# The last 64 rows of wq to 64 partitions, and the gate's weights in one transfer

## The chip, the cores and the metric

The kernel runs on one core of one Trainium2 chip. The metric is the device time of one execution in microseconds (us); lower is better. The times given are medians of several runs of the same program on the same chip, and the profile is of one further execution.

## The reference, cut to what matters

One decode step: attention of one query token over a cache of 65,536 positions (16 query heads, 8 key and value heads of size 256), mixed by a gate with a small token mixer.

```
x = A_x                                              # (1, 1, 448)
g = sigmoid((x * gate_w).sum(-1, keepdims=True))     # gate_w has 448 numbers

q = (x @ wq).reshape(16 heads, 256)                  # wq: 448 x 4096
p = softmax(q . k_cache * 256 ** -0.5)               # k_cache, v_cache: 8 x 65536 x 256, bf16
a = (p . v_cache) @ wo                               # wo: 4096 x 448

h = layernorm(x)
u = gelu(einsum("bsd,sf->bdf", h, w1) + b1)          # 448 x 1792
b = transpose(einsum("bdf,fs->bds", u, w2) + b2)

out = g * a + (1 - g) * b                            # 448 numbers, bf16
```

Keys and values are 268 MB each. They are read once and make up nearly all the bytes.

## The kernel before, in words

**The stream.** Keys and values are cut into 32 blocks (8 heads, 4 blocks each) of 16,384 positions. A block is 8.39 MB: 128 partitions with 128 rows of 256 numbers each, that is 64 KB in a row per partition. `load_k_whole` (line 132) fetches a block of K into two of the three slots of `k_all`, `load_v` (line 135) a block of V into `vt`. All these loads are issued on SyncE's queue. The loop (line 608 in the profile is the loop and the code that opens its stages) handles two blocks a round: transposes of K on VectorE (line 413), scores on PE (421), a running softmax (478 to 517), products with V on PE (441). In each round `load_wo_wide` (144) fetches 224 KB of wo to every fourth partition. After the loop the last two blocks are written out by hand, the last V block in seven pieces that get smaller (`LAST`, line 161), and the result is stored (708).

**Ahead of the loop.** The query is computed from wq, which lies in `vt` until the first V block takes its place. Rows 0 to 383 are `wq_m`, three rows to each of 128 partitions (issued at line 170). The last 64 rows are `wq_t` (issued at 167): each row of 4096 numbers is cut into two halves, so that 128 half rows of 4 KB fill 128 partitions. A partition then holds the half `half` of a row, and the 16 heads fall into two halves of 8. So that each head's product takes only the rows of its own half, x for these rows is prepared in two columns, `xtm`: x's last 64 numbers are written twice in a row (`xrr`, line 231, VectorE), a matmul with a one turns them into a column (240, PE), and a multiplication with the mask `par` (203), which is 1 on the partitions of the right parity, makes the two columns (248). The query's matmuls are at lines 300 (`wq_m`, three for each of 32 columns) and 307 (`wq_t`, one for each).

ScalarE's queue carries the small inputs: x (`xr`, line 166), three tables of the mixer (`tables`, 176), the gate's weights in two halves of 448 bytes (`gw`, 178), and `b2b` (181). The tables are turned by one matmul (262) and copied to `wb1` (272). VectorE makes the layernorm from a broadcast of x over all partitions (the matmul at 244; 265 to 284), with `veps` at 268. ScalarE computes 14 gelus (289) and the gate's exponential (351). Then the loop begins.

**What sets the order.** A helper, `seq`, ties every instruction to the one before it on the same engine, so each engine and each queue runs in the order in which the code is written. The framework adds the waits for data. It also gives each transfer outside the loop one of eight completion counters in turn; a transfer that takes a counter for the second time waits until the first one that used it has landed. The ten transfers ahead of the loop are x, wq_t, the three tables, wq_m, gw, gw, b2b and the first K block.

Of the kernel before, what the change touches and what calls it, by code (L numbers as in the profile page):

```python
# [8 lines left out]
FP32 = mybir.dt.float32  # L9
BF16 = mybir.dt.bfloat16  # L10
ACT = mybir.ActivationFunctionType
ALU = mybir.AluOpType
AXIS = mybir.AxisListType

HQ = 16
HKV = 8
DH = 256
REP = HQ // HKV
# [15 lines left out]
def kernel(  # L34
# [15 lines left out]
    nc = tc.nc  # L50

    D = A_x.shape[-1]
# [10 lines left out]
    def seq(ins):  # L63
        e = ins.ins.engine
        if e in last:
            tc.add_manual_dep(
                ins.ins,
                last[e],
                mybir.DependencyInfo(
                    mybir.DependencyClass.NoSync, mybir.DependencyReason.DATA  # L70
                ),
                reason="program order",
            )
        last[e] = ins.ins.name
        return ins

    kvpool = ctx.enter_context(tc.tile_pool(name="kvpool", bufs=1))
    const = ctx.enter_context(tc.tile_pool(name="const", bufs=1))
# [8 lines left out]
    vt = kvpool.tile([128, VP, DH], BF16, name="vt")  # L87
# [17 lines left out]
    xr = const.tile([1, D], BF16)  # L105
    gw = const.tile([1, D], BF16)
# [2 lines left out]
    b2b = const.tile([1, 1], BF16)  # L109
    DM = 384  # L110
    wq_m = vt[:, 0:48, :].rearrange("p a b -> p (a b)").rearrange("p (k n) -> p k n", k=3)
    wq_t = vt[:, 48:56, :].rearrange("p a b -> p (a b)")
    early = slots[2].rearrange("p j d -> p (j d)")
    gel = [early[:, b * D:(b + 1) * D] for b in range(NF)]
    early_f = early[:, NF * D:].bitcast(FP32)
# [43 lines left out]
    def load_v_last(n):  # L159
# [4 lines left out]
            ))  # L164

    seq(nc.scalar.dma_start(out=xr[:], in_=A_x[0, 0].rearrange("(o n) -> o n", o=1)))
    seq(nc.sync.dma_start(
        out=wq_t[:, :], in_=A_wq[DM:D, :].rearrange("r (h n) -> (r h) n", h=2)
    ))
    seq(nc.sync.dma_start(out=wq_m, in_=A_wq[0:DM, :].rearrange("(p k) n -> p k n", k=3)))  # L170
    for k, table in enumerate((
        B_w1[0].rearrange("(b p) -> b p", p=128),
# [1 line left out]
        B_w2.rearrange("(b p) o -> b (p o)", p=128),  # L174
    )):
        seq(nc.scalar.dma_start(out=tables[k * NF:(k + 1) * NF, :], in_=table))
    for n0, n1 in ((0, D // 2), (D // 2, D)):
        seq(nc.scalar.dma_start(
            out=gw[:, n0:n1], in_=gate_w.rearrange("(o n) -> o n", o=1)[:, n0:n1]
        ))  # L180
    seq(nc.scalar.dma_start(out=b2b[:], in_=B_b2.rearrange("(o n) -> o n", o=1)))
    load_k_whole(0, 0)

# [5 lines left out]
    ident_f = const.tile([128, 128], FP32)  # L189
# [4 lines left out]
        out=val[:], in_=rowsel[:, :, :, 0:NI], op=ALU.add, axis=AXIS.XY  # L194
# [3 lines left out]
        out=fst[:],  # L198
        in_=ident_f[:].rearrange("p (a i r) -> p i r a", a=4, r=REP)[:, 0:2],
        op=ALU.add, axis=AXIS.X,  # L200
    ))
    par = const.tile([128, REP], FP32)
    seq(nc.vector.tensor_reduce(
        out=par[:], in_=ident_f[:].rearrange("p (a r) -> p r a", r=REP), op=ALU.add, axis=AXIS.X
    ))
    nval = const.tile([128, REP], FP32)
    seq(nc.scalar.mul(out=nval[:], in_=val[:], mul=-scale))
# [6 lines left out]
        out=same[:], in_=val[:].unsqueeze(1).to_broadcast([128, 64, REP])  # L214
# [8 lines left out]
        out=sel[:],  # L223
        in_=ident.rearrange("p (w k) -> p w k", w=NW).unsqueeze(2).to_broadcast([128, NW, NQ, 32]),
# [1 line left out]


    xm = const.tile([128, 3], BF16)
    xtm = const.tile([128, REP], BF16)
    xrr = const.tile([1, D - DM, 2], BF16)  # L230
    seq(nc.vector.tensor_copy(
        out=xrr[:], in_=xr[:, DM:D].unsqueeze(2).to_broadcast([1, D - DM, 2])
    ))
    x_col = hd_ps[:, 40:44]
    for k in range(3):
        seq(nc.tensor.matmul(
            x_col[:, k:k + 1], lhsT=xr[:, 0:DM].rearrange("o (p k) -> o k p", k=3)[:, k, :],
            rhs=ones_b[:, 0:1], start=True, stop=True,
        ))
    seq(nc.tensor.matmul(  # L240
        x_col[:, 3:4], lhsT=xrr[:].rearrange("o a r -> o (a r)"),
        rhs=ones_b[:, 0:1], start=True, stop=True,
    ))
    seq(nc.tensor.matmul(
        sm_ps[:, 0:D], lhsT=ones_b[:, :], rhs=xr[:, :], start=True, stop=True
    ))
    seq(nc.vector.tensor_copy(out=xm[:], in_=x_col[:, 0:3]))
    seq(nc.vector.tensor_scalar(
        out=xtm[:], in0=par[:], scalar1=x_col[:, 3:4], scalar2=None, op0=ALU.mult
    ))  # L250


    stats = work.tile([128, nc.vector.BN_STATS_DIM], FP32)
# [9 lines left out]
        t_ps, lhsT=tables[:, :], rhs=ident[0:3 * NF, 0:3 * NF], start=True, stop=True  # L263
# [5 lines left out]
        out=veps[:], in0=mv[:, 1:2], scalar1=1e-5, scalar2=None, op0=ALU.add  # L269
# [5 lines left out]
    for _ in range(2):  # L275
        seq(nc.vector.scalar_tensor_tensor(
            out=ntmp[:], in0=rstd[:], scalar=rstd[:, 0:1], in1=veps[:],
            op0=ALU.mult, op1=ALU.mult,
        ))
        seq(nc.vector.tensor_scalar(  # L280
            out=ntmp[:], in0=ntmp[:], scalar1=-0.5, scalar2=1.5, op0=ALU.mult, op1=ALU.add
# [3 lines left out]
        out=h_bc, in0=xf, scalar1=mv[:, 0:1], scalar2=rstd[:, 0:1],  # L285
        op0=ALU.subtract, op1=ALU.mult,
    ))
    for b in range(NF):
        seq(nc.scalar.activation(
            out=gel[b], in_=h_bc, func=ACT.Gelu_apprx_tanh,  # L290
# [2 lines left out]

    q_ps = hd_ps[:, 0:2 * HQ]
    for h in range(HQ):
        half, hh = divmod(h, HQ // 2)
        for c in range(2):
            col = c * HQ + h
            for k in range(3):
                seq(nc.tensor.matmul(  # L300
                    q_ps[:, col:col + 1],
                    lhsT=wq_m[:, k, h * DH:(h + 1) * DH].rearrange("p (d c) -> p c d", c=2)[:, c, :],
                    rhs=xm[:, k:k + 1],
                    start=(k == 0),
                    stop=False,
                ))
            seq(nc.tensor.matmul(
                q_ps[:, col:col + 1],
                lhsT=wq_t[:, hh * DH:(hh + 1) * DH].rearrange("p (d c) -> p c d", c=2)[:, c, :],
                rhs=xtm[:, half:half + 1],  # L310
                start=False,
                stop=True,
            ))
# [3 lines left out]
    for w in range(NW):  # L317
        seq(nc.tensor.matmul(
            qq_ps[:, w * 2 * HQ:(w + 1) * 2 * HQ],
            lhsT=sel[:, w, :, :].rearrange("p a k -> p (a k)"), rhs=qb[:],  # L320
# [3 lines left out]
    for k in range(2):  # L324
        seq(nc.vector.tensor_copy(
            out=qq[:, :, :, k, :], in_=qq_ps.rearrange("p (w g r) -> p w g r", g=HKV, r=REP)
# [316 lines left out]
    for n in (L - 1, L):  # L643
# [14 lines left out]
        else:  # L658
            def rest_base():
# [9 lines left out]
                out=lsv[:], in0=val[:], scalar1=lsum[:, 0:1], scalar2=None, op0=ALU.mult  # L669
# [8 lines left out]
                out=rdv[:], in0=rdv[:], scalar1=gcol[:, 0:1], scalar2=None, op0=ALU.mult  # L678
# [6 lines left out]
    for c in range(2):  # L685
        for e in range(2):
            seq(nc.tensor.matmul(
                o_last[:, c, :],
                lhsT=acc[:, e, :].rearrange("p (d c) -> p c d", c=2)[:, c, :],
                rhs=fst[:, e, :],  # L690
# [4 lines left out]
        out=oT[:], in0=o_last, in1=rdv[:].unsqueeze(1).to_broadcast([128, 2, REP]), op=ALU.mult  # L695
    ))
    for r in range(REP):
        for c in range(2):
            for k in range(2):
                seq(nc.tensor.matmul(  # L700
                    f_rows[k], lhsT=oT[:, c, r:r + 1],
                    rhs=wo_sb[:, r, c, k * MC:(k + 1) * MC],
# [36 lines left out]
```

## Time and profile before

| | |
|---|---|
| median of 3 runs | 1263.77 us (1263.45 to 1264.1) |
| the profiled execution: its time | 1264.05 us |
| its span, first to last instruction | 1262.3 us |
| moved | 544.35 MB, mean 431 GB/s |
| TensorE clock granted, mean | 0.817 |
| busy share of the span | PE 65%, VectorE 56%, PE's weight loads 26%, ScalarE 6%, GpSimd 1% |

The profile is of one execution. Its time is 1.75 us more than its span; the difference lies around the first and the last instruction. Times in rows of the timeline count from the span's start. A row of the timeline gives start, duration, engine, line, operation, output and inputs, how many, and in brackets how long the engine sat idle before it and what ended that. "q" behind an engine's name is its sequencer, which issues DMAs; the duration of such a row is that of the issue, not of the transfer. The DMA share is the mean busy share of the core's 16 DMA engines; since a packet is counted where its time falls or ends, a short stretch can show more than 1.

### The profile page before, as it was taken

The numbers are of one execution on the slowest core, as the hardware profiler recorded it, in microseconds if no ns is written. First come the engines' busy times: TensorE is split into PE (matmuls) and PEld (weight loads), VectorE is DVE, ScalarE is ACT, GpSimd is POOL, SyncE is SP. The second block draws the span as 40 slices with busy tenths as digits, with TensorE's granted clock in tenths as the row PEclk, the third lists the DMA queues.
The fourth block names the chain that finished last, engine by engine and source line by source line (L and its number), as shares of the span: only waits on it lengthen the run. The fifth ranks groups of instructions, "written<-read, shape, count | busy, mean of one in ns | idle before, by whom it ended". The sixth has DMA issues, their size and how long they took to land.

```text
span 1262.3 us, 12389 instructions
## 1 busy us (share of the span) xinstructions
PE 816.7 (65%) x4818; PEld 329.8 (26%) x4818; DVE 705.4 (56%) x733; ACT 78.2 (6%) x170; POOL 7.7 (1%) x21
## 2 busy tenths in 40 slices
PE   5757567574676756677564766658666586565668
PEld 2222222231222212222222322213222132222224
DVE  3665456664556644566444665446654456654575
ACT  5000000000000000000000000000000000000000
POOL 2000000000000000000000000000000000000000
PEclk8787788778888877878779887788887788877979
DMA  9999999999999999999999999999999999999998
GB/s 416 432 435 432 439 432 432 439 432 427 438 438 418 447 416 436 430 437 436 435 432 439 432 432 439 432 439 432 432 439 432 439 432 432 439 432 435 423 431 357
DMA packets 11623, 544.35 MB, mean 431 GB/s; under 512 B 1532, under 2 KB 1918, under 8 KB 2782
## 3 DMA queue, kind: packets, MB, share of 16 engines
q1 hardware_dynamic: 11522, 544.22, 99.6%
q8 instruction: 6, 0.10, 0.0%
q10 hardware_dynamic: 92, 0.01, 0.0%
q14 instruction: 3, 0.02, 0.0%
HBM read 544.22 MB, written 0.00 MB: 431 GB/s over the span
## 4 chain that ended last, share of the span: by engine, by line
DMA 69%; PE 13%; DVE 12%; issue 4%; SPq 0%; ACT 0%; DVEq 0%
DMA k_all<-in_A_k_cache_dram 67%; PE sc L421 12%; DVE kT L413 12%; DMA k_all<-in_A_v_cache_dram 2%; PE pv_last L566 0%; PE hd_ps L557 0%; PE f L566 0%; PE f L700 0%; PE sm_ps L543 0%; PE hd_ps L466 0%; ACT p_sb L509 0%; DVE rmax L478 0%; SPq L132 0%; PE hd_ps L543 0%; PE sm_ps L496 0%
## 5 line engine op out<-in xcount | busy, mean ns | idle before, releaser
L421 PE MATMUL sc<-kT,qz 128*128 128x512 bf16 x2048 | 546.8, 417 | 324.4 <-DVE kT L413 324.3
L413 DVE STREAM_TRANSPOSE kT<-k_all 128x2048 f32<-128x2048 f32 x256 | 570.9, 2283 | 211.6 <-DMA k_all<-in_A_k_cache_dram 161.1
L421 PEld LDWEIGHTS <-qz 128*128 128x128 bf16 x2048 | 211.7, 103 | 658.3 <-issue 479.6
L441 PE MATMUL pv_ps<-vt,pT 128*4 128x512 bf16 x1968 | 166.9, 513 | 27.3 <-DVE pT L516 27.3
L522 DVE SCALAR_TENSOR_TENSOR acc<-acc,al,pv_ps 128x512 f32<-128x512 f32 x31 | 23.2, 747 | 155.4 <-PE pv_ps L441 155.4
L441 PEld LDWEIGHTS <-pT 128*4 128x4 bf16 x2000 | 55.7, 106 | 125.9 <-issue 77.1
L509 ACT ACTIVATE p_sb<-sc,nb 128x512 bf16<-128x512 f32 x32 | 22.0, 687 | 1023.6 <-DVE nb L505 1023.6
L478 DVE TENSOR_REDUCE rmax<-sc 128x1 f32<-128x512 f32 x32 | 22.1, 691 | 63.7 <-PE sc L421 63.7
L516 DVE STREAM_TRANSPOSE pT<-p_sb 128x512 bf16<-128x512 bf16 x32 | 22.8, 711 | 27.1 <-ACT p_sb L509 27.1
L528 PE MATMUL hd_ps<-lsum,same 128*128 128x1 f32 x30 | 7.6, 322 | 28.8 <-DVE lsum L517 28.8
L496 PE MATMUL sm_ps<-mrun,ones_f 1*128 1x2 f32 x64 | 12.1, 257 | 21.2 <-DVE mrun L495 13.0
L482 PE MATMUL sm_ps<-ident_f,rmax 128*1 128x128 f32 x32 | 8.6, 270 | 24.6 <-DVE rmax L478 24.6
L566 PE MATMUL pv_last<-wo_in,steps 128*128 128x448 bf16 x64 | 15.6, 368 | 3.8 <-PEq L608 3.8
L566 PEld LDWEIGHTS <-steps 128*128 128x128 bf16 x128 | 11.6, 101 | 20.9 <-issue 12.7
L561 DVE TENSOR_TENSOR a_acc<-a_acc,hd_ps 1x448 f32<-1x448 f32 x15 | 9.1, 609 | 14.0 <-PE hd_ps L557 14.0
L496 PEld LDWEIGHTS sm_ps<-mrun,ones_f 1*128 1x128 f32 x64 | 9.4, 183 | 27.5 <-DVE mrun L495 16.4
L557 PE MATMUL hd_ps<-wo_sb,oT 128*1 128x448 bf16 x60 | 16.4, 365 | 0.0
L570 ACT CAST wo_sb<-pv_last 128x448 bf16<-128x448 f32 x16 | 8.5, 532 | 122.5 <-PE pv_last L566 122.5
L566 PE MATMUL f<-wo_in,steps 128*128 128x448 bf16 x64 | 15.5, 367 | 0.0
L573 ACT COPY wo_sb<-wo_sb 128x896 bf16<-128x896 bf16 x15 | 14.1, 937 | 15.3 <-PE hd_ps L557 15.3
L528 PEld LDWEIGHTS hd_ps<-lsum,same 128*128 128x128 f32 x30 | 6.3, 262 | 30.1 <-DVE lsum L517 30.1
L553 DVE CAST oT<-hd_ps 128x2 bf16<-128x2 f32 x15 | 2.4, 159 | 21.0 <-PE hd_ps L543 21.0
(123 smaller groups left out, 196.1 us busy)
## 6 DMA issues: line engine op xcount, KB each, us to landing
k_all<-in_A_k_cache_dram SPq DMA_DIRECT2D x2, 4096.0 KB, 15.9
vt<-in_A_v_cache_dram SPq DMA_DIRECT2D x1, 5120.0 KB
k_all<-in_A_v_cache_dram SPq DMA_DIRECT2D x1, 4096.0 KB
wo_in<-in_A_wo_dram SPq DMA_DIRECT2D x15, 224.0 KB, 27.8
vt<-in_A_wq_dram SPq DMA_DIRECT2D x1, 3072.0 KB, 10.4
vt<-in_A_v_cache_dram SPq DMA_DIRECT2D x1, 3072.0 KB
k_all<-in_A_v_cache_dram SPq DMA_DIRECT2D x1, 2048.0 KB
k_all<-in_A_v_cache_dram SPq DMA_DIRECT2D x1, 1024.0 KB, 22.3
```

What stands on the lines that cost most here:

```text
L413: seq(nc.vector.transpose(out=kT_tiles[i % 2][:].rearrange("p j w k c -> p (j w k c)").bitcast(FP32), in_=slots[pair[i // 4]][:, i % 4 * N ...
L421: seq(nc.tensor.matmul(sc_tiles[e][:, :], lhsT=qz[:, 2 * w + c, 2 * (NI - i):2 * (NI - i) + 128], rhs=kT_tiles[i % 2][:, :, w, :, c], star ...
L441: seq(nc.tensor.matmul(dst[32 * grp:32 * grp + 2 * REP, :, :], lhsT=pT[:, 32 * jj + 2 * REP * ip:32 * jj + 2 * REP * (ip + 1)], rhs=pairs( ...
L478: seq(nc.vector.tensor_reduce(out=rmax[:], in_=sc_ps[:, :], op=ALU.max, axis=AXIS.X))
L496: seq(nc.tensor.matmul(sm_ps[:, 128:128 + REP], lhsT=ones_f[0:1, :], rhs=mrun[0:1, :], start=True, stop=True))
L509: seq(nc.scalar.activation(out=p_sb[:, :], in_=sc_ps[:, :], func=ACT.Exp, scale=scale, bias=nb[:, 0:1], accum_out=den[:, 0:1],))
L516: seq(nc.vector.transpose(out=pT[:, :], in_=p_sb[:, :]))
L522: seq(nc.vector.scalar_tensor_tensor(out=acc[:], in0=acc[:], scalar=al_tiles[e][:, 0:1], in1=src[:, :, :], op0=ALU.mult, op1=ALU.add,))
L528: seq(nc.tensor.matmul(hd_ps[:, 460:461], lhsT=same[:].rearrange("p a r -> p (a r)"), rhs=lsum[:, 0:1], start=True, stop=True,))
L557: seq(nc.tensor.matmul(a_ps, lhsT=oT[:, c, r:r + 1], rhs=wo_sb[:, r, c, :], start=(r == 0 and c == 0), stop=(r == REP - 1 and c == 1),))
L566: seq(nc.tensor.matmul(wo_ps[c], lhsT=steps[:, WS - u:WS - u + 128], rhs=wo_in[:, 2 * u + c, :], start=(u == 0), stop=(u == WS - 1),))
L573: seq(nc.scalar.copy(out=wo_sb[:, 0], in_=wo_sb[:, 1]))
```

## The change

The last 64 rows of wq are loaded as they are: 64 rows of 8 KB to partitions 0 to 63, in twice the columns of `vt`. The contraction over them then needs one column of x, `xt`, on 64 partitions: x goes into its matmul directly, and the copy `xrr`, the mask `par` and the multiplication fall away. The 32 query matmuls at what was line 307 contract over 64 rows instead of 128. The gate's weights come in one transfer of 896 bytes instead of two of 448. There are nine transfers ahead of the loop instead of ten.

```diff
+    DT = D - DM
-    wq_t = vt[:, 48:56, :].rearrange("p a b -> p (a b)")
+    wq_t = vt[0:DT, 48:64, :].rearrange("p a b -> p (a b)")
...
-    seq(nc.sync.dma_start(
-        out=wq_t[:, :], in_=A_wq[DM:D, :].rearrange("r (h n) -> (r h) n", h=2)
-    ))
+    seq(nc.sync.dma_start(out=wq_t, in_=A_wq[DM:D, :]))
...
-    for n0, n1 in ((0, D // 2), (D // 2, D)):
-        seq(nc.scalar.dma_start(
-            out=gw[:, n0:n1], in_=gate_w.rearrange("(o n) -> o n", o=1)[:, n0:n1]
-        ))
+    seq(nc.scalar.dma_start(out=gw[:], in_=gate_w.rearrange("(o n) -> o n", o=1)))
...
-    par = const.tile([128, REP], FP32)
-    seq(nc.vector.tensor_reduce(
-        out=par[:], in_=ident_f[:].rearrange("p (a r) -> p r a", r=REP), op=ALU.add, axis=AXIS.X
-    ))
...
-    xtm = const.tile([128, REP], BF16)
-    xrr = const.tile([1, D - DM, 2], BF16)
-    seq(nc.vector.tensor_copy(
-        out=xrr[:], in_=xr[:, DM:D].unsqueeze(2).to_broadcast([1, D - DM, 2])
-    ))
+    xt = const.tile([DT, 1], BF16)
...
-        x_col[:, 3:4], lhsT=xrr[:].rearrange("o a r -> o (a r)"),
+        x_col[0:DT, 3:4], lhsT=xr[:, DM:D],
...
-    seq(nc.vector.tensor_scalar(
-        out=xtm[:], in0=par[:], scalar1=x_col[:, 3:4], scalar2=None, op0=ALU.mult
-    ))
+    seq(nc.vector.tensor_copy(out=xt[:], in_=x_col[0:DT, 3:4]))
...
-        half, hh = divmod(h, HQ // 2)
...
-                lhsT=wq_t[:, hh * DH:(hh + 1) * DH].rearrange("p (d c) -> p c d", c=2)[:, c, :],
-                rhs=xtm[:, half:half + 1],
+                lhsT=wq_t[:, h * DH:(h + 1) * DH].rearrange("p (d c) -> p c d", c=2)[:, c, :],
+                rhs=xt[:, 0:1],
```

## The prediction

> **What bounds the kernel now.** I read the page first: the rate of the transfers slice by slice, the queues, the chain that ended last.
>
> ```profile
> span 1262.3 us, 12389 instructions
> GB/s 416 432 435 432 439 432 432 439 432 427 438 438 418 447 416 436 430 437 436 435 432 439 432 432 439 432 439 432 432 439 432 439 432 432 439 432 435 423 431 357
> q1 hardware_dynamic: 11522, 544.22, 99.6%
> DMA 69%; PE 13%; DVE 12%; issue 4%; SPq 0%; ACT 0%; DVEq 0%
> ```
>
> The rate is flat from the second slice to the last but one, and SyncE's queue q1 alone takes 99.6% of what the 16 DMA engines could give. So I asked for busy times in a few long stretches (columns: stretch, busy time and count of PE, PEld, DVE, ACT, POOL, then PEclk, DMA share, GB/s).
>
> ```profile
> 2.00:30.00 28.00, 14.55 (x168) 8.22 (x168) 9.31 (x35) 17.03 (x26) 6.24 (x12) 0.87 1.01 430
> 30.00:1257.00 1227.00, 799.64 (x4611) 320.02 (x4611) 695.50 (x696) 60.87 (x143) 0.00 (x0) 0.82 1.00 434
> 1257.00:1262.30 5.30, 2.47 (x48) 1.54 (x44) 0.54 (x2) 0.34 (x1) 0.00 (x0) 0.63 0.11 38
> ```
>
> The DMA share is 1.00 for 1227 us at 434 GB/s and 1.01 in the opening. So the time is: about 2 us until data flow, 1255 us of an unbroken stream, 5.3 us of tail. The last pieces of the chain show that the tail hangs on the stream:
>
> ```profile
> 1236.10 21.67 DMA k_all<-in_A_v_cache_dram
> 1257.77 0.05 issue
> 1257.81 0.55 PE hd_ps L466 x12
> ```
>
> The last piece of V lands at 1257.77, and PE starts 0.04 us later. What lengthens the stream by 1 us ends the kernel 1 us later; what engines save beside it is worth nothing, unless it keeps the stream from running dry. I therefore read when SyncE issues, and how long a load lies in the queue (us from issue to landing).
>
> ```profile
> 0.73 0.42 SPq L167 DMA_DIRECT2D vt<-in_A_wq_dram  x1
> 1.21 0.41 SPq L170 DMA_DIRECT2D vt<-in_A_wq_dram  x1
> 4.16 0.33 SPq L132 DMA_DIRECT2D k_all<-in_A_k_cache_dram  x1
> 25.51 0.36 SPq L135 DMA_DIRECT2D vt<-in_A_v_cache_dram  x1
> 43.38 0.34 SPq L132 DMA_DIRECT2D k_all<-in_A_k_cache_dram  x1
> ...
> k_all<-in_A_k_cache_dram SPq DMA_DIRECT2D x31, 27.9
> vt<-in_A_wq_dram SPq DMA_DIRECT2D x1, 512.0 KB, 3.4
> wo_in<-in_A_wo_dram SPq DMA_DIRECT2D x15, 224.0 KB, 27.8
> ```
>
> A block of K is 8.39 MB, 19.3 us at 434 GB/s, and takes 27.9 us: it lies some 8.6 us behind others. In the loop the stream has that much cover. The thinnest cover is at the start: wq and the first K block are 3.67 + 8.39 = 12.06 MB, and 2:30 moved 28 x 0.430 = 12.04 MB, so they are in at about 30; V's first block is issued at 25.51.
>
> **The change, part by part.** *The transfer of 64 rows.* 524,288 bytes in both forms; at 434 GB/s they hold the stream for 1.21 us. Half as many packets of twice the size could save something; what small packets cost at most is seen at the end, where V comes in rows of 1 to 4 KB:
>
> ```profile
> 1252.00:1254.00 2.00, 2.00 (x49) 0.96 (x42) 0.64 (x4) 0.00 (x0) 0.00 (x0) 1.00 0.96 406
> ```
>
> 406 against 434 GB/s is 7%, of 1.21 us that is 0.1 us: the gain lies between 0 and 0.1, and I take 0.05. On the other side, the rows now go to partitions 0 to 63 alone. If the rate of a transfer goes with the half of the partitions that it reaches, 512 KB hold the stream for 2.42 us, 1.21 more; wq's other rows, behind it in the same queue, come that much later. Lower bound 0, upper bound 1.21. The nearest row is wo_in: 32 partitions only, and 27.8 us to landing where K, issued just ahead of it, takes 27.9, so a transfer to few partitions did not stretch. But its rows go to every fourth partition from 0 to 124, so it does not show what the lower half alone does. No transfer of the trace does. I take 1.2, since a load into one half leaves the part of SBUF that lies behind the other half without writes, and the next transfer waits in each engine's order. By the wo_in row taken at its word it would be 0, and I keep that as a rival.
>
> The Trainium skill has a rule for this (SBUF — State Buffer, "Door 1: The DMA port swizzle"): partitions 0 to 63 reach only 8 of the 16 ports through which transfers write, so such a tile loads at about half the rate of 128 partitions. By its 218 GB/s the transfer would take 2.4 us, an estimate, and the sum would be the same +1.2; no run here shows it yet.
>
> *The K block's issue.* The first K load waits before it is issued, on a transfer with which it shares no data:
>
> ```profile
> SPq L132 <- DMA vt<-in_A_wq_dram: 2.5, 1, 2.5
> 2.04 0.24 PE L236 MATMUL hd_ps<-ones_b,xr 1*128 1x1 bf16 x3 [2.04 <-DMA xr<-in_A_x_dram]
> ```
>
> Transfers ahead of the loop take eight completion counters in turn. This load is the tenth, so it shares its counter with the second, wq's last rows. With one transfer fewer it is the ninth and shares it with x, which is in at 2.04: issue at about 2.1 in place of 4.16. Its data still come behind wq's other rows (issued at 1.21), so the stream gains nothing: 0. After the loop nothing moves to another load: each still waits for the eighth before it.
>
> *VectorE and PE ahead of the loop.* These rows carry it:
>
> ```profile
> 0.74 0.53 ACTq L166 DMA_DIRECT2D xr<-in_A_x_dram  x1
> 2.12 0.41 ACTq L176 DMA_DIRECT2D tables<-in_B_w_dram  x1
> 2.56 0.58 ACTq L178 DMA_DIRECT2D gw<-in_gate_w_dram  x2
> 5.34 0.27 DVE L203 TENSOR_REDUCE par<-ident_f 128x2 f32<-128x128 f32 x1
> 6.66 1.66 DVE L231 COPY xrr<-xr 1x128 bf16<-1x128 bf16 x1
> 8.42 0.53 PE L244 MATMUL sm_ps<-xr,ones_b 1*128 1x448 bf16 x1
> 9.93 0.19 PE L262 MATMUL hd_ps<-steps,tables 42*128 42x42 bf16 x1 [0.98 <-DMA tables<-in_B_w_dram]
> 10.53 0.15 DVE L268 TENSOR_SCALAR veps<-mv 128x1 f32<-128x1 f32 x1
> 10.60 0.18 DVE L272 COPY wb<-hd_ps 128x28 f32<-128x28 f32 x1
> 12.97 9.23 ACT L289 ACTIVATE k_all<-k_all,wb 128x448 bf16<-128x448 f32 x14 [0.75 <-DVE k_all L284]
> 23.51 0.20 ACT L351 ACTIVATE ez<-z 1x1 f32<-1x1 f32 x1
> 32.50 4.49 DVE L413 STREAM_TRANSPOSE kT<-k_all 128x2048 f32<-128x2048 f32 x2
> ```
>
> Gone are the reduction to par (0.27), the copy to xrr (1.66) and one issue on ScalarE (half of 0.58). xr feeds its matmul directly, so L240 and L244 run soon after 2.04. VectorE's chain to veps then ends 0.3 + 0.3 + 1.7 = 2.3 us earlier at best. But wb waits for L262, and that for the tables, which came at 9.93 on ScalarE's queue: wb at 9.93 + 0.19, about 10.15 in place of 10.60. The 14 gelus, the exponential and the loop's entry move up by that 0.45. Nothing of it reaches the end: V's first block is then issued at 25.05, with wq and K still flowing until 30. The cover is 30 - 25.51, less the 1.3 us that x took from issue (0.74) to landing (2.04): about 3.2 us now, 3.6 then, and 4.8 if the stream is 1.2 later. Should it be gone, each us by which V comes late is a us at the end. The 32 matmuls with 64 rows in place of 128 come after wq's first rows and run beside the gelus: 0.
>
> *gate_w.* One packet fewer of 448 bytes: under 0.05 us of one DMA engine, 0.
>
> **Sum.** The profiled execution took 1264.05 us: 1262.3 of span and 1.75 around it. 1264.05 + 1.2 - 0.05 = 1265.2. The median of the three runs is 1263.77, 0.28 below the profiled one, so the forecast in medians is 1263.77 + 1.15 = 1264.9. That is 0.09%; a measurement of this kernel can tell about 0.2% (2.5 us) from no change.
>
> **The rivals.** *The half load costs nothing.* For it: wo_in's 27.8 beside K's 27.9. Against it: those rows are spread over all partitions. Then only the packets count: 1263.77 - 0.05 = 1263.7.
>
> *The tables come late, and the stream runs dry before V (slower).* The small transfers of ScalarE share the DMA engines with SyncE's: the last of the three tables is issued at 2.12 to 2.53 and all are in at 9.93, 7.4 us later for 10.5 KB, which fits turns between wq's rows of 24 KB (24,576 bytes at 434/16 = 27.1 GB/s: 0.9 us a turn). Now K's rows of 64 KB (2.4 us a turn) are in the queue 2 us sooner, and wq's last rows fill four places of each engine, not eight. Each turn that the tables take behind K instead of wq costs 1.5 us. Gelus, exponential and V's issue follow; from 3.6 us of net delay on the stream runs dry. All six turns (three transfers, data and completion): 9 - 0.45 - 3.6 = 5 us, 1268.7; over 0.2% it needs more than four. Against it: wq's eight rows an engine lie ahead of K's in the same queue in either kernel, and the tables are issued before K.
>
> The same skill (DMA: Bandwidth & Descriptors, "Queues, rings and completion order") says that each DMA engine goes round the queues that have work, a packet at a time; by that rule the tables would keep their place between wq's rows and this rival would be worth nothing. The 7.4 us above agree with it.
>
> *It is faster by over 0.2%.* That would need 2.5 us out of opening or tail: the opening's 2 us are one transfer's first latency and the tail isn't touched. Nothing in the profile gives it.
>
> **How the numbers follow.** Half rate: 0.55, 1264.5 to 1265.4. No cost: 0.32, 1263.4 to 1264.1. Late tables: 0.09, from 1264 to 1268.7, of it 0.06 over 0.2%. Something unseen: 0.04, half on each side. So faster 0.02, within 0.2% 0.90, slower 0.08. The range from 1263.2 to 1266.0 takes in the first two cases whole, with 0.3 us for runs, and the milder part of the third.
>
> **What would show it.** wq's 512 KB land 1.2 us later after their issue (4.6 in place of 3.4 us) under the forecast, 3.3 under the first rival; wq's first matmul starts at about 12.8 or 11.6 (now 11.7). The first K load is issued at about 2.1. wb starts near 10.15, and V's first issue is near 25.05. The stretch 30:1257 stays at 434 GB/s. The second rival would show the tables' matmul at 13 or later, V's first issue past 29, and a hole in the GB/s between 30 and 35. Wrong altogether would be a median under 1261.2 or over 1266.3, or a loop in which the DMA share falls below 1.00.

## The result, and the profile after

The changed kernel takes 1267.24 us (median of 9 runs, 1266.94 to 1267.7) where the kernel before takes 1263.72 (9 runs, 1263.45 to 1264.19): the ratio is 1.0027, with a 95% interval of 1.0019 to 1.0036. It is 3.5 us slower. The forecast was 1264.9, with a range up to 1266.0. The prediction held that a measurement can tell about 0.2% from no change; this interval is 0.09% to either side, and the loss of 0.27% is clear of it. The profiled execution took 1266.94 us, its span is 1265.5.

The page of the changed kernel, and its long stretches (columns as in the prediction):

```profile
span 1265.5 us, 12386 instructions
q1 hardware_dynamic: 11458, 544.22, 99.4%
```

```profile
0.00:2.00 2.00, 0.00 (x0) 0.00 (x0) 0.00 (x0) 0.00 (x0) 1.44 (x10) 1.00 0.00 0
2.00:30.00 28.00, 17.92 (x166) 12.07 (x166) 7.07 (x33) 16.89 (x26) 6.24 (x12) 1.00 1.04 429
30.00:1257.00 1227.00, 797.39 (x4565) 318.86 (x4565) 695.71 (x697) 61.07 (x144) 0.00 (x0) 0.82 1.00 433
```

The stream is as unbroken as before: a DMA share of 1.00 for 1227 us. The loss is not in the loop. SyncE's issues and the two landings of wq:

```profile
0.74 0.60 SPq L168 DMA_DIRECT2D vt<-in_A_wq_dram  x1
1.39 0.57 SPq L169 DMA_DIRECT2D vt<-in_A_wq_dram  x1
2.02 0.41 SPq L133 DMA_DIRECT2D k_all<-in_A_k_cache_dram  x1
27.99 0.35 SPq L136 DMA_DIRECT2D vt<-in_A_v_cache_dram  x1
```

```profile
vt<-in_A_wq_dram SPq DMA_DIRECT2D x1, 3072.0 KB, 11.4
vt<-in_A_wq_dram SPq DMA_DIRECT2D x1, 512.0 KB, 4.7
```

The 512 KB land 4.7 us after their issue, where it was 3.4. So the opening does what was forecast (4.6), and the stream ends later. Now the tail, from the last step of the attention to the store of the result; first the changed kernel, then the kernel before:

```profile
1259.25 0.16 DVE L679 TENSOR_TENSOR oT<-hd_ps,rdv 128x4 bf16<-128x4 f32 x1 [3.62 <-PE hd_ps L451]
1260.05 0.38 DVE L691 CAST res<-f 1x224 bf16<-1x224 f32 x1 [0.64 <-PE f L685]
1260.90 0.32 SPq L693 DMA_DIRECT2D out_dram<-res  x1
```

```profile
1258.68 0.16 DVE L694 TENSOR_TENSOR oT<-hd_ps,rdv 128x4 bf16<-128x4 f32 x1 [4.26 <-PE hd_ps L466]
1259.84 0.38 DVE L706 CAST res<-f 1x224 bf16<-1x224 f32 x1 [1.00 <-PE f L700]
1260.30 0.32 SPq L708 DMA_DIRECT2D out_dram<-res  x1
```

`oT` is 0.57 us later; the last copy ends at 1260.43 in place of 1260.22, only 0.21 later. The other 0.36 lies in the products between `oT` and the copy: they took 0.55 us in place of 0.91, at a granted clock of 1.00 in the stretch 1259:1260, where the kernel before had 0.50. But the store is issued 0.47 us behind the end of that copy, where it was 0.08. And from the end of the store's issue (1261.22) to the program's end (1265.5) it is 4.3 us, where it was 1.7. What lies there shows in the view by source line of line 719 (734 in the kernel before), the `with` around the whole program, to which the closing barrier of all engines is booked; in that barrier each engine waits until the others have finished (the columns: an engine's event instructions, how many, their shortest, median and longest ns, and when the first and the last of them started). The changed kernel, then the kernel before:

```profile
L719 DVEq EVENT_SEMAPHORE  x2: 21/21/21, 1262.5 to 1265.5; - x2
L719 PEldq EVENT_SEMAPHORE  x2: 51/51/51, 1262.5 to 1263.0; - x2
```

```profile
L734 DVEq EVENT_SEMAPHORE  x2: 21/21/21, 1261.7 to 1262.2; - x2
L734 PEldq EVENT_SEMAPHORE  x2: 51/51/51, 1261.7 to 1262.2; - x2
```

All engines do their last step at 1263.0 in the changed kernel, but VectorE does its own at 1265.5. There is nobody left to wait for: the others have passed the same barrier. So of the 3.2 us that the span grew, 0.2 lie ahead of the last copy's end (0.57 less the 0.36 of the products), 0.5 between that and the barrier, most of it ahead of the store, and 2.5 in one late instruction of VectorE, behind all the work.

The two programs differ in length. Counted in the compiled programs, VectorE has 203 instructions in the kernel before and 200 in the changed one (`par`, `xrr` and a wait fewer), and SyncE 97 and 98 (one wait more, in the part behind the loop). That gave the theory that I took to the chip: **where a program ends** decides, through the blocks in which instructions come (theory "end"), beside the half rate of the prediction. The rival was that all of it follows from the later and differently timed stream (theory "stream").

### The profile page after: what moved, and what is told of

Same layout as the page of the kernel before. It is cut to its first block, busy times and chain, and to the rows that moved or that the text cites. A ratio compares the mean times of both kernels' runs of the same rounds, so it can differ in the third digit from the quotient of the medians.

```text
span 1265.5 us, 12386 instructions
## 1 busy us (share of the span) xinstructions
PE 818.1 (65%) x4818; PEld 333.3 (26%) x4818; DVE 703.3 (56%) x731; ACT 78.3 (6%) x170; POOL 7.7 (1%) x21
## 4 chain that ended last, share of the span: by engine, by line
DMA 69%; PE 14%; DVE 12%; issue 4%; ACT 0%; SPq 0%; DVEq 0%; ACTq 0%
DMA k_all<-in_A_k_cache_dram 69%; PE sc L406 13%; DVE kT L398 12%; PE hd_ps L451 0%; PE pv_last L426 0%; DVE rmax L463 0%; DMA xr<-in_A_x_dram 0%; PE hd_ps L672 0%; ACT p_sb L494 0%; PE pv_ps L426 0%; PE sm_ps L481 0%; DVE pT L501 0%; SPq L133 0%; PE f L685 0%; PE sm_ps L467 0%
## 5 line engine op out<-in xcount | busy, mean ns | idle before, releaser
L463 DVE TENSOR_REDUCE rmax<-sc 128x1 f32<-128x512 f32 x32 | 22.1, 692 | 63.6 <-PE sc L406 63.6
```

What stands on the lines that cost most here:

```text
L463: seq(nc.vector.tensor_reduce(out=rmax[:], in_=sc_ps[:, :], op=ALU.max, axis=AXIS.X))
```

## The experiments

Every comparison is with the kernel before on the same chip: 1263.77 us in the first group of runs (27 runs), 1263.87 in the second (33), 1263.85 in the third (15), 1263.96 in the last (15). Experiments 1 to 4 are the first group, 5 to 8 the second, 9 to 11 the third, 12 the last; a difference between two groups is uncertain by the 0.1 to 0.2 us by which the kernel before moves.

**1. VectorE's program as long as before.** The changed kernel with three one-element fills.

```diff
+    spare = const.tile([1, 1], FP32)
+    for _ in range(3):
+        seq(nc.vector.memset(spare[:], 0.0))
```

> The changed kernel with three one-element memsets more on VectorE in the opening, so that VectorE's program has as many instructions as before the change (203 in place of 200). Theory 'end': in the changed kernel VectorE takes its last step 2.5 us after all other engines because the program's last instructions have moved against the blocks in which they are fetched; then the last event of VectorE falls back to about 0.05 us around the others' and the time is 1267.2 - 2.5 = 1264.7. Theory 'stream' (all of the 3.5 us comes from the opening's transfers and is passed down the stream): no change, 1267.2.

Measured: 1265.49 us (1265.22 to 1266.51), ratio 1.0014 (1.0005 to 1.0023).

```profile
L722 DVEq EVENT_SEMAPHORE  x2: 21/21/21, 1263.1 to 1263.5; - x2
L722 PEldq EVENT_SEMAPHORE  x2: 51/51/51, 1263.1 to 1263.5; - x2
```

Three more instructions, and the kernel is 1.75 us faster: VectorE's last step comes with the others'. It is less than the 2.5 us of the trace, and the two profiled executions show why. The time outside the span is 1.46 us in the changed kernel and 1.78 in experiment 1 (1.46 to 1.56 in all four kernels whose very last step is late, 1.78 to 1.88 in all others), so some 0.3 us of a step that is late alone costs nothing. And the last copy of experiment 1 ended at 1260.99, 0.56 later: its data came 0.2 later, and its last products ran at a granted clock of 0.50 (stretch 1259:1260) where the changed kernel's ran at 1.00. Whether the runs that weren't profiled differ in clock in the same way isn't shown.

**2. One instruction instead of three.**

> The changed kernel with one memset more on VectorE (201 instructions). Theory 'end': if only the very last instruction fell into the next block, one more would push one or two more of them over the edge and the delay stays about 2.5 us (1267.2), or the edge lies the other way and it vanishes (1264.7); either tells where the edge is. Theory 'stream': 1267.2, with no late VectorE.

Measured: 1268.0 us (1267.68 to 1270.03), ratio 1.0036 (1.0022 to 1.005). It is slower than with none.

```profile
L722 DVEq DRAIN  x2: 124/268/412, 1260.7 to 1265.9; - x2
L722 PEldq EVENT_SEMAPHORE  x2: 51/51/51, 1263.1 to 1266.2; - x2
```

With 201 instructions it is VectorE's last step but one that comes late, at 1265.9, and now the whole barrier waits for it: PE's last step moves to 1266.2. The late place moves through the program by one step for one instruction.

**3 and 4. The half rows back.** The changed kernel with wq's last rows loaded in halves to 128 partitions, as before; in 4 with the three fills too. The products read other rows of wq in their place.

```diff
-    wq_t = vt[0:DT, 48:64, :].rearrange("p a b -> p (a b)")
+    wq_t = vt[0:DT, 0:16, :].rearrange("p a b -> p (a b)")
+    wq_h = vt[:, 48:56, :].rearrange("p a b -> p (a b)")
...
-    seq(nc.sync.dma_start(out=wq_t, in_=A_wq[DM:D, :]))
+    seq(nc.sync.dma_start(
+        out=wq_h, in_=A_wq[DM:D, :].rearrange("r (h n) -> (r h) n", h=2)
+    ))
```

> The changed kernel with wq's last rows loaded as before, 128 half rows of 4 KB to 128 partitions; the query's fourth product takes wq's first rows in place of them, so the query isn't the reference's. Everything else is as changed, VectorE's program has 200 instructions. Theory 'half rate' (64 rows to the lower partitions hold the stream about 1.1 us longer): the 512 KB land 3.4 us after issue in place of 4.7, and the time is 1267.2 - 1.1 = 1266.1, with VectorE still late by 2.5. Theory 'the 64 rows cost nothing': 1267.2.

> Both: 128 half rows (with the same part of the query replaced) and three memsets more on VectorE. Theories 'end' and 'half rate' together, if they add: 1267.2 - 2.5 - 1.1 = 1263.6, as before the change. 'Stream' alone: 1266.1 or 1263.7 according to the transfer only, the same as the run with the half rows and no memsets.

Measured: 1266.77 us (1266.25 to 1267.0), ratio 1.0023 (1.0014 to 1.0032), and with the fills 1264.38 (1264.23 to 1264.96), 1.0005 (0.9996 to 1.0014).

```profile
vt<-in_A_wq_dram SPq DMA_DIRECT2D x1, 512.0 KB, 3.4
vt<-in_A_wq_dram SPq DMA_DIRECT2D x1, 3072.0 KB, 10.6
```

That is kernel 4: the landing is back at 3.4. With VectorE's end put right, the half rows are worth 1.1 us (1265.49 - 1264.38), which is the price of the load of 64 rows measured there. What is left of 4 above the kernel before, 0.6 us, is about the 0.4 us by which SyncE's store is still late. Without the fills the half rows are worth only 0.5 (1267.24 - 1266.77), and the fills are worth 2.4 on the half rows (1266.77 - 1264.38) where they were worth 1.75. So the effects don't simply add, and the 1266.1 that I expected of 3 was missed by 0.7. The profiled execution of 3 shows `oT` 0.26 us earlier than in the changed kernel (1258.98), but its last products ran at a granted clock of 0.50 in place of 1.00, and its last copy ended 0.10 later (1260.52); VectorE's last step was late by 2.4 us as before. Whether that clock accounts for the 0.6 us between the two prices in the medians isn't shown.

**5. A shorter VectorE program, and no transfer changed.** The kernel before, with three VectorE instructions given to other engines.

```diff
-    seq(nc.vector.memset(pv_ps[:], 0.0))
-    seq(nc.vector.memset(pv_last[:], 0.0))
...
+    for t in (pv_ps, pv_last):
+        seq(nc.scalar.copy(out=t[:], in_=wo_in[:, 0:2, 0:DH]))
...
-    seq(nc.vector.tensor_copy(
+    seq(nc.gpsimd.tensor_copy(
```

> The kernel before, with all its transfers and its query as they were, and three instructions fewer on VectorE (200 in place of 203): the two memsets of the sums are done by ScalarE from a zero tile, the copy to xrr by GpSimd. Theory 'end': VectorE's last event comes about 2.5 us after the other engines' and the time rises from 1263.8 to about 1266.1, although not one transfer and nothing in the loop is changed. Theory 'stream': 1263.8.

Measured: 1265.94 us (1265.63 to 1266.65), ratio 1.0017 (1.0008 to 1.0026).

```profile
L734 DVEq EVENT_SEMAPHORE  x2: 21/21/21, 1261.7 to 1264.8; - x2
L734 PEldq EVENT_SEMAPHORE  x2: 51/51/51, 1261.7 to 1262.2; - x2
```

The theory "stream" falls here. All the loads are those of before, and of the three instructions taken from VectorE only the copy to `xrr` is one that the change took; its last step is late by 2.6 us all the same, and the kernel 2.1 us slower (1265.94 - 1263.87).

**6. The 64 rows on every second partition.** Experiment 1, with the rows on partitions 0, 2, ... 126, so that they are spread over both halves. The products read other rows in their place.

```diff
+    wq_e = vt[0:128:2, 48:64, :].rearrange("p a b -> p (a b)")
...
-    seq(nc.sync.dma_start(out=wq_t, in_=A_wq[DM:D, :]))
+    seq(nc.sync.dma_start(out=wq_e, in_=A_wq[DM:D, :]))
```

> The changed kernel with three memsets more on VectorE (first experiment, 1265.5), and the 64 rows of 8 KB sent to every second partition, 0 to 126, instead of to 0 to 63; the query's fourth product takes wq's first rows instead, so the query isn't the reference's. Theory 'half rate by the lower half': the rate follows which partitions are written, so rows spread over all of them cost no more than 128 half rows: 512 KB in 3.4 us and 1265.5 - 1.1 = 1264.4. Theory 'fewer partitions' (64 rows of 8 KB cost it wherever they go): 4.7 us, 1265.5.

Measured: 1264.99 us (1264.57 to 1265.41), ratio 1.0009 (1.0 to 1.0018).

```profile
0.74 0.59 SPq L169 DMA_DIRECT2D vt<-in_A_wq_dram  x1
```

```profile
vt<-in_A_wq_dram SPq DMA_DIRECT2D x1, 512.0 KB, 3.7
```

```profile
0.00:2.00 2.00, 0.00 (x0) 0.00 (x0) 0.00 (x0) 0.00 (x0) 1.44 (x10) 1.00 0.00 0
```

These are the issue, the landing and the first 2 us. The landing falls from 4.9 in experiment 1 to 3.7, so the lower half is what stretched it. The time falls by only 0.5, though; 0.6 above the half rows remain. Some of that can be named: the issue of 64 rows takes 0.59 us where that of 128 half rows took 0.42, and the first packet of data starts at 2.2 us where it started at 1.8 in experiment 4, which had a DMA share of 0.13 up to 2 us. That is one loss of 0.4 us, seen twice. The rest I leave open; experiment 6 ran in another group than 1 and 4.

**7. The gate's weights alone.** The kernel before, with that one edit of the change.

```diff
-    for n0, n1 in ((0, D // 2), (D // 2, D)):
-        seq(nc.scalar.dma_start(
-            out=gw[:, n0:n1], in_=gate_w.rearrange("(o n) -> o n", o=1)[:, n0:n1]
-        ))
+    seq(nc.scalar.dma_start(out=gw[:], in_=gate_w.rearrange("(o n) -> o n", o=1)))
```

> The kernel before with only the gate's weights in one transfer. The first K block then waits for x instead of for wq's last rows (issue near 2 us). VectorE has 202 instructions, SyncE 98 in place of 97. Theory 'end': SyncE's stall of 0.4 us, which before lay behind the result's store, lies ahead of it (the store is issued 0.48 in place of 0.08 us after the result's last copy), so 1263.8 + 0.4 = 1264.2, more if VectorE's third step from the end is late. Theory 'stream': 1263.8.

Measured: 1265.07 us (1264.56 to 1265.67), ratio 1.001 (1.0001 to 1.0019).

```profile
L731 DVEq EVENT_SEMAPHORE  x2: 21/21/21, 1262.8 to 1263.1; - x2
L731 ACTq EVENT_SEMAPHORE  x2: 17/17/17, 1262.0 to 1263.1; - x2
```

One transfer fewer costs 1.2 us. VectorE has one wait fewer (202 instructions), and now its last step but two is late, by 0.8 us against ScalarE's, and the others wait for it. SyncE has one instruction more (98), and its store is issued 0.48 us behind the last copy, as in the changed kernel.

**8. SyncE's end moved as well.** Experiment 1, with the transfer of `b2b` issued on SyncE's queue behind the first K block (SyncE 99).

```diff
-    seq(nc.scalar.dma_start(out=b2b[:], in_=B_b2.rearrange("(o n) -> o n", o=1)))
...
+    seq(nc.sync.dma_start(out=b2b[:], in_=B_b2.rearrange("(o n) -> o n", o=1)))
```

> The changed kernel with three memsets more on VectorE (1265.5) and the transfer of b2b moved from ScalarE's to SyncE's queue, behind the first K block, which gives SyncE 99 instructions in place of 98. Theory 'end': SyncE's stall moves one instruction ahead of the store's own, into a wait of 11 us, and the store is issued 0.1 us after the last copy: 1265.5 - 0.4 = 1265.1. If the stall of 0.4 us is the store's own, 1265.5.

Measured: 1264.96 us (1264.53 to 1266.64), ratio 1.001 (1.0001 to 1.0019).

```profile
1260.99 0.38 DVE L694 CAST res<-f 1x224 bf16<-1x224 f32 x1 [1.00 <-PE f L688]
1261.47 0.26 SPq L696 DMA_DIRECT2D out_dram<-res  x1
```

The store follows the copy by 0.10 us again, and the time falls by 0.5. What is left above the kernel before, 1.1 us, is the load of 64 rows.

**9 and 10. Longer by 125 or 128.** The kernel before, with that many fills on VectorE in the opening (the edit of 9; 10 has 128 in its place).

```diff
+    spare = const.tile([1, 1], FP32)
+    for _ in range(125):
+        seq(nc.vector.memset(spare[:], 0.0))
```

> The kernel before with 125 one-element fills added to VectorE's program behind its last two summing steps of the query's preparation; no transfer is changed, and what is computed stays. VectorE's program is 125 instructions longer than before's, which is as far from before's as the changed kernel's (three fewer) if instructions come in blocks of 128. Theory of blocks: VectorE's last step of the closing barrier is late again by some 2.5 us, the time about 1265.9 (as where VectorE was made three shorter: 1265.9). Rival, that only a shorter program is late, or that it hung on the three removed steps: 1263.8, like the kernel before. The 125 fills of about 0.06 us take some 8 us before the query's matmuls are ready or beside them; in the changed kernel a query that was 5 us later was hidden; if these are not, both theories come out later by that, which shows in the first pass of the loop and not at the closing barrier.

> The same with 128 fills, three more. Theory of blocks: VectorE's end lies where it lay in the kernel before, and its last step is not late: about 1263.8. Rival, that a longer program is always or never late: the same time as with 125 fills. What the fills themselves cost in the first pass is the same for both, so the difference of the two (2.1 us by the theory of blocks, 0 by the rival) is the reading.

Measured: 1270.62 us (1269.92 to 1271.29), ratio 1.0053 (1.0039 to 1.0067), and 1269.33 (1269.08 to 1269.8), 1.0044 (1.003 to 1.0058). The closing barrier of 9, and VectorE's part of it in 10:

```profile
L737 DVEq EVENT_SEMAPHORE  x2: 21/21/21, 1266.5 to 1269.3; - x2
L737 PEldq EVENT_SEMAPHORE  x2: 51/51/51, 1266.5 to 1266.9; - x2
```

```profile
L737 DVEq EVENT_SEMAPHORE  x2: 21/21/21, 1266.8 to 1267.2; - x2
```

With 125 more the last step is late by 2.4 us, with 128 more it is not. Both kernels are 5 us slower for a reason of their own, which the expectation had left open. A fill took 0.113 us, not 0.06, and V's first block waited for them (kernel 9):

```profile
17.67 7.21 DVE L602 MEMSET spare<- 1x1 f32 x64
33.22 0.35 SPq L135 DMA_DIRECT2D vt<-in_A_v_cache_dram  x1
```

```profile
30.00:40.00 10.00, 6.24 (x20) 3.44 (x21) 1.64 (x20) 2.00 (x3) 0.00 (x0) 1.00 0.74 295
```

The stream runs dry between 30 and 40 (share 0.74): this is the price of the prediction's second rival, brought about by the fills. V is issued 7.71 us later than before and `oT` starts 4.74 later (1263.42), so the cover was 2.97 us; the prediction worked out 3.2. The medians of 9 and 10 differ by 1.3 us where 2.1 was expected; the spans differ by 2.0, with the stream of 9 ending 0.3 earlier, and the time outside the span is 1.6 us in 9 and 1.8 in 10.

**11. The gate's transfer with both ends put right.** Experiment 7 with `b2b` on SyncE's queue (SyncE 100) and one fill (VectorE 203).

> The kernel before with the gate's weights in one transfer, b2b's transfer issued on SyncE's queue behind the first K (SyncE three instructions longer than before's, two longer than with the one transfer alone), and one one-element fill on VectorE (its program as long as before's). Theory of program ends: one transfer for the gate costs nothing itself, the time is about 1263.8 (1263.4 to 1264.2), no late VectorE step, the result's store about 0.1 us behind the last copy. Rival, that the one transfer of the gate (16 KB, and the first K 0.4 us sooner) costs time of its own: about 1265.0 as with the one transfer alone (1265.07).

Measured: 1263.90 us (1263.62 to 1264.38), ratio 1.0 (0.9991 to 1.0009). The whole 1.2 us of experiment 7 is gone. The one transfer, and the first K block issued at 1.68 us instead of 4.16, cost nothing and bring nothing.

**12. Longer by 61.**

> As with 125 fills, but 61: VectorE's program is then as far from the kernel before's (three fewer) as the changed kernel's, if what decides repeats every 64 instructions, and not if it repeats every 128. The fills took 0.114 us each from 17.7 us on, so 61 of them end near 24.7 and hold nothing up. Blocks of 128: no late step of VectorE at the closing barrier, about 1263.9. Period of 64: VectorE's last step late by 2.4 to 2.6 us again, about 1265.9. A third, that any longer program is late, also gives 1265.9, though with 128 fills VectorE was not late.

Measured: 1264.14 us (1263.5 to 1264.55), ratio 1.0 (0.9991 to 1.0009).

```profile
L737 DVEq EVENT_SEMAPHORE  x2: 21/21/21, 1262.2 to 1262.6; - x2
L737 PEldq EVENT_SEMAPHORE  x2: 51/51/51, 1262.2 to 1262.6; - x2
```

VectorE's last step comes with PE's. The period is not 64, and a longer program is not late as such.

## Why the prediction was wrong

**The failed step: the tail.** The prediction put the tail at nothing: "the tail isn't touched", "After the loop nothing moves to another load", and "0" for the gate's weights in one transfer. It read this off the work alone. The removed instructions were priced by their duration and place in the opening, where they cost nothing; that they also move the end of an engine's program had no term in the sum and no rival. The transfer that was put at 0 cost 1.2 us by itself (experiment 7), all of it through the ends of two programs (experiment 11), and behind the loop SyncE has one wait more than before.

The runs give the terms, in medians. Taken off one after the other: VectorE's late step 1.75 us (changed kernel to experiment 1), SyncE 0.5 (experiments 1 to 8), the load of 64 rows 1.1 (experiment 8 to the kernel before), in all 3.4 of the 3.5 us. That they add up is no check, since each begins where the one before it ended. In the other order the load is 0.5 (changed kernel to 3), the late step 2.4 (3 to 4) and the rest 0.6; on the kernel before a late step cost 2.1 (experiment 5). So the late step is worth 1.75 to 2.4 us and the load 0.5 to 1.1, though two pairs agree on 1.1 (1 and 4, 8 and the kernel before). Both low prices are differences from the changed kernel itself, which is some 0.6 us faster than the sum of its parts; why stays open. In either order at least 2.2 us of the loss have nothing to do with how wq is loaded.

**The half load: right in its landing, with luck in its size.** +1.2 was forecast; 1.1 was measured with VectorE's end put right, 0.5 with the late step; 4.6 us to landing, 4.7 measured. But in experiment 6 the lower half accounts for about half of the 1.1, and the 64-row form for the other, 0.4 us by its later first data; that second part was priced at nothing, or at a gain of 0.05. That two costs add up to the 1.2 of one is luck. The first rival, no cost, is out by experiments 1 and 4. The rule of the Trainium skill that the prediction weighed (SBUF — State Buffer, "Door 1: The DMA port swizzle") agrees with the landings: 4.7 to 5.4 us on partitions 0 to 63 (changed kernel, 1, 2 and 8), 3.7 on every second partition, 3.4 to 3.6 on all. In time it was worth 0.5 us, not the 1.2 of an estimate from its figure.

**The first K block: right.** Issue at 2.02 (2.1 forecast), and nothing gained; experiment 11 shows the early issue without the load of 64 rows. **wb and V's first issue.** The rows of the changed kernel's opening, then two of the kernel before:

```profile
10.18 0.19 PE L248 MATMUL hd_ps<-steps,tables 42*128 42x42 bf16 x1 [7.28 <-DMA tables<-in_B_w_dram]
12.85 0.24 PE L285 MATMUL hd_ps<-xm,vt 128*128 128x1 bf16 x3 [2.48 <-DMA vt<-in_A_wq_dram]
13.02 0.18 PE L292 MATMUL hd_ps<-xt,vt 64*128 64x1 bf16 x1
13.14 0.24 PE L285 MATMUL hd_ps<-xm,vt 128*128 128x1 bf16 x3
22.13 0.19 DVE L300 CAST qb<-hd_ps 128x32 bf16<-128x32 f32 x1 [9.57 <-PE hd_ps L292]
```

```profile
11.70 0.24 PE L300 MATMUL hd_ps<-xm,vt 128*128 128x1 bf16 x3 [1.57 <-DMA vt<-in_A_wq_dram]
11.82 0.22 PE L300 MATMUL hd_ps<-xm,vt 128*128 128x1 bf16 x3
```

The tables came 0.25 us later than before, and wq's first matmul starts at 12.85 (12.8 forecast). Then comes a cost that was put at 0: the 32 groups of four matmuls take 0.29 us each where they took 0.11, so the query is ready at 22.1 and V is issued at 27.99 instead of the 25.05 forecast. It stays hidden for the reason that the prediction gave, the cover of about 3 us and the later stream: the share stays at 1.00. **Late tables, slower (the second rival):** not what happened. Experiment 9, with fills in place of late tables, shows that a late V does run the stream dry, and from nearly the point that was worked out. **Faster:** nothing gave it.

## What to carry to other kernels

When an edit adds or removes instructions, compare the closing barrier of both kernels by engine as well as the work: an engine whose last steps come late there, with nothing to wait for, is worth microseconds that no instruction's duration shows. Test it by adding a few harmless instructions to that engine's program before blaming the edit's own work. And when several causes are taken off one by one, take them off in a second order too: the prices here changed by 0.6 us. And price a load by the partitions it reaches and by its issue, each with its own experiment.

## What the runs showed of the hardware

**The end of a program has a price that goes with its length.** How late VectorE's late step started, against the others in the same barrier, and how long the store waited behind the last copy on SyncE:

| VectorE's instructions | kernels | late step |
|---|---|---|
| 203, 331, 264 | before, 1, 4, 6, 8, 11 (203), 10 (331), 12 (264) | none |
| 202 | 7 | last but two, 0.8 us |
| 201 | 2 | last but one, 2.7 us, and all wait |
| 200, 328 | changed, 3, 5 (200), 9 (328) | last, 2.4 to 2.6 us |

| SyncE's instructions | kernels | store behind the last copy |
|---|---|---|
| 97 | before, 5, 9, 10, 12 | 0.08 us |
| 98 | changed, 1, 2, 3, 4, 6, 7 | 0.46 to 0.48 us |
| 99, 100 | 8, 11 | 0.06 to 0.10 us |

For VectorE it repeats with 128 instructions (328 is late as 200 is, 331 is not as 203 is not) and not with 64 (264 is not late). That the late step is the first of a block of instructions that has yet to be fetched isn't proved, but the trace's packets point to it. All the packets that q14, one of the two instruction queues, moves within the span have 8,192 bytes; in the compiled program VectorE's 203 instructions are 12,992 bytes, 64 each, so that such a packet holds 128 of them, the period found. In the changed kernel one of them moves between the two last steps of VectorE's barrier (8 GB/s for 1 us is 8 KB, and no engine is busy):

```profile
1263.00:1264.00 1.00, 0.00 (x0) 0.00 (x0) 0.00 (x0) 0.00 (x0) 0.00 (x0) 0.50 0.03 8
```

It starts at 1263.58, and the late step follows 1.4 us behind its end. So it is in all six late runs (changed, 2, 3, 5, 7, 9): a packet starts 1.0 us behind VectorE's last instruction ahead of the late step (counted from that instruction's start, in 7 from its end), and the late step starts 1.2 to 1.4 us behind the packet's end. The page's rows of this queue (packets, MB, share), first of the changed kernel, then of experiment 1, go with it:

```profile
q14 instruction: 2, 0.02, 0.0%
```

```profile
q14 instruction: 3, 0.02, 0.0%
```

The changed kernel doesn't fetch less: its third packet of the tail starts at 1266.21, behind the span's end, where experiment 1 had all three in by 1262.6. Which engine's program a packet holds the trace doesn't say.

The Trainium skill (Runtime: NRT & Kernel Launch, "Instruction fetch mechanics") says that instructions are refilled in blocks of 256 and that crossing a boundary is mostly hidden. Here the period is 128, and at the end of the program up to 2.7 us were not hidden. SyncE's 0.4 us came and went with its length too, but its period was not tried and its cause is open: in the changed kernel no packet of an instruction queue moves between the last copy's end (1260.43) and the store (1260.90).

**Matmuls with 64 and with 128 rows in turn** took 0.29 us for a group of four with 128 columns of weights, 0.11 with 128 rows throughout (the rows of lines 285, 292 and 300 above). Why isn't shown.
